# Integer-add weight conversion, a new order of the attention steps, and expert steps inside the last attention units, in a fused attention and two-expert-layer kernel

## The chip, the cores and the metric

The kernel runs on one core of a Trainium2 chip. The metric is the device time of one execution in microseconds (us); the shown time is the median of three runs. One more execution was taken with the hardware profiler, and every duration below comes from it. The engines are PE (matrix multiply; PEld is its weight load), DVE (vector), ACT (scalar, activation), POOL (general purpose) and SP, whose queue starts nearly all DMA transfers.

## The reference

Causal attention with a compressive memory is followed by two feed-forward layers; all three are computed in float32 or better.

```python
B, H, S, D = (4, 8, 576, 64)
scores = scale * np.matmul(q, k.transpose(0, 1, 3, 2))      # causal mask, softmax -> a
local = np.matmul(a, v)
mem_out = einsum(phi(q), M_prev) / (einsum(phi(q), z_prev) + 1e-06)
attn = g * mem_out + (1 - g) * local                        # g = sigmoid(beta) by head
x = attn.transpose(0, 2, 1, 3).reshape(2304, 512)
h = x @ w_in;   x1 = (h * np.cos(h)) @ w_out                # w_in 512 x 2048, w_out 2048 x 512
h = x1 @ w2_in; out = (np.maximum(h, 0.0) ** 2) @ w2_out
```

The four weight matrices are float64. The kernel gets them as pairs of 32-bit words and makes float32 of them itself.

## The kernel before, in words

**Attention** is 16 units (4 batches by 4 pairs of heads). A unit's instructions are written out by hand: `CFG['order']` is a list of tokens such as `S1/2` or `c7/0`. One pass of the loop over u at the end of `attention` (`for u in range(first, end)`) goes through the list, and token T/d issues part T for unit u+d. `_Pinned` keeps each engine's instructions in exactly this order. S are the score matmuls (tile `sps`), R the masked row maxima (tiles `P`, `mx`), E the exponentials, Ns the sums (`sm`), Np the normalisation of P, PT the transposes (`ptps`, `PT`), V and PV the products with the values (`o`), q1 to q6 and qp the memory branch, X the result's way out (`x<-o`, then a store to `xT` in DRAM). In the profile all of these have line L47, that of `_Pinned`, so they are told apart by tile.

**One weight block is converted in each unit**, tokens c1 to c9. `c_load` brings a 128 x 512 block of float64 words (tile `wraw`, two buffers), and `c_steps` has seven operations: absolute value of the high word (ACT), clamp (DVE in attention, POOL later), shift and mask (DVE), sign (DVE, tile `wb`), the exponent (DVE, `wa<-wb`), low word times exponent (DVE, `wa<-wraw,wa`), and the add of the two (POOL, `wa<-wa,wb`). Eight of the 16 blocks are split into a high and a low part that stay on chip, eight are stored to DRAM.

**The expert layers** (`moe`) are 160 steps s, 80 for each layer, one block of up to 512 tokens and 128 hidden columns each. `l1` does 12 matmuls into tile `h`; `g_a` to `g_g` do the activation on ACT and DVE and split it into `gh` and `gl`; `l2`, 12 matmuls, follows two steps later (`SK`). Here no order is pinned: a scheduler sets each engine's order. Between the steps run the conversions of the remaining 48 blocks, one per step for the first layer's last 16 blocks, then blocks of the second layer at `CFG['rate']` = 0.2 per step (these are stored to DRAM, tiles `ws2in` and `ws2out`, and brought back later), and the rest one per step from s = 64 on. The scheduler moves the conversions that have a rate up: 11 of them run in the stretch from 344 to 417 us, through two buffers of `wa` and `wb`. `store` frees a buffer when its transfer has landed.

**The hand-over.** The first expert block's four x parts (`load_x`: `x_load`, then `x_split` with `xh` on ACT, `xl` on DVE) are loaded and split at the end of the pass u = 12. The first `l1` can be issued after `attention` has returned, and the four `h` buffers of `ps_h` lie in space that the attention's pools give back.

Of the kernel before, what the change touches and what calls it, by code (L numbers as in the profile page):

```python
# [32 lines left out]
class _Pinned:  # L33
# [5 lines left out]
    def __getattr__(self, name):  # L39
# [16 lines left out]
CFG = {'order': """  # L56
    R1/1 S0/1 PT1/0 V1/0 Np2/0 PT0/0 c8/-1 R0/1 q5/0 E1/1 q6/0 S2/1 q1/1 PV0/-1 PV3/-1 c2/0 PV2/-1
    E0/1 V0/0 R2/1 PV4/-1 Ns0/1 PV1/-1 PT2/0 S3/1 PT3/0 q2/1 c3/0 V2/0 c4/0 c9/-1 PT4/0 c5/0 qpT/0
    E2/1 R3/1 mem/-1 q3/1 V3/0 Np0/1 Np1/1 V4/0 PT5/0 q4/1 E3/1 c6/0 qpV/0 c7/0 PT6/0 V5/0 X/-1 V6/0
    Ns1/1 S1/2 c1/1 Np3/1  # L60
""",
       'pt': 'AAAAADD',
       'norm': 'PPPA',
       'qpt': 'A',
       'x': 'A',
       'whi': 'A',
       'NA': 4,
       'rate': [0, 0.2, 0.2, 0.2],
       'short': 3,
       'order2': [0, 1, 2, 4, 3],  # L70
       'warm': 8,
       'skew': 2,
       'segs': [[0, 0, 8], [1, 0, 16], [0, 8, 16]],
# [4 lines left out]
def kernel(  # L78
# [62 lines left out]

    def c_steps(raw, clamp=None):
# [4 lines left out]
        af, bf = a.bitcast(F32), b.bitcast(F32)  # L147
# [81 lines left out]

    def attention(ctx):  # L230
        ae = ctx.enter_context(tc.tile_pool(name="ae", bufs=2))
        ac = ctx.enter_context(tc.tile_pool(name="ac", bufs=1))
        a2 = ctx.enter_context(tc.tile_pool(name="a2", bufs=2))
        ps_s = ctx.enter_context(tc.tile_pool(name="ps_s", bufs=2, space=PSUM))
        ps_t = ctx.enter_context(tc.tile_pool(name="ps_t", bufs=2, space=PSUM))
# [394 lines left out]
    def moe(ctx, g_p, g_3):  # L630
        ps_h = ctx.enter_context(tc.tile_pool(name="psh", bufs=4, space=PSUM))
        ps_a = ctx.enter_context(tc.tile_pool(name="psa", bufs=1, space=PSUM))
        hs, rs, kis, gs, acc = {}, {}, {}, {}, {}
        order2 = CFG["order2"]
        segs = [(1, j, a, e) for j, a, e in CFG["segs"]]
        segs += [(1, j, 0, NF) for j in range(2, NB)] + [(2, j, 0, NF) for j in order2]
        steps = [(p, j, f) for p, j, a, e in segs for f in range(a, e)]
        opens = {(p, j, a) for p, j, a, e in segs}
        closes = {(p, j, e - 1) for p, j, a, e in segs}
        xneed, s0 = {}, 0  # L640
        for p, j, a, e in segs:
            if a == 0 and s0:
                for kk in range(KD):
                    xneed.setdefault(max(s0 - 10 + 2 * kk, 0), []).append((p, j, kk))
            s0 += e - a
        part = {}

        def l1(s):
            p, j, f = steps[s]
            n = blocks[j][1]  # L650
            hi, lo = wt[p, "in", f]
            h = ps_h.tile([128, 512], F32, tag="h", name="h")
            for kk in range(KD):
                xh, xl = xt[p, j, kk]
                for x, (lt, rt) in enumerate(((hi, xh), (hi, xl), (lo, xh))):
                    nc.tensor.matmul(  # L656
                        out=h[:, 0:n],
                        lhsT=lt[:, kk * 128:(kk + 1) * 128],
                        rhs=rt[:, 0:n],
                        start=(kk == 0 and x == 0),  # L660
                        stop=(kk == KD - 1 and x == 2),
                    )
            hs[s] = h[:, 0:n]

# [265 lines left out]
```

## Time and profile before

| | |
|---|---|
| runs, us | 1063.88, 1065.28, 1070.35; median 1065.28 |
| profiled execution, us | 1069.46, of which the span is 1067.7 |
| PE busy | 1014.9 us, 95% |
| DVE busy | 700.0 us, 66% |
| ACT busy | 543.6 us, 51% |
| POOL busy | 352.9 us, 33% |
| mean granted PE clock | 0.99 |

The profile's overview cuts the span into 40 slices. PE is at nine tenths or more in nearly all of them, but DVE is at nine tenths in the first fifth of the span, and again from about 600 to 700 us, and PE dips to eight tenths around the hand-over and in the stretch with conversions. So the program has stages with different limits, and each has to be read by itself.

### The profile page before, as it was taken

The numbers are of one execution on the slowest core, as the hardware profiler recorded it, in microseconds if no ns is written. First come the engines' busy times: TensorE is split into PE (matmuls) and PEld (weight loads), VectorE is DVE, ScalarE is ACT, GpSimd is POOL, SyncE is SP. The second block draws the span as 40 slices with busy tenths as digits, with TensorE's granted clock in tenths as the row PEclk, the third lists the DMA queues.
The fourth block names the chain that finished last, engine by engine and source line by source line (L and its number), as shares of the span: only waits on it lengthen the run. The fifth ranks groups of instructions, "written<-read, shape, count | busy, mean of one in ns | idle before, by whom it ended". The sixth has DMA issues, their size and how long they took to land.

```text
span 1067.7 us, 14438 instructions
## 1 busy us (share of the span) xinstructions
PE 1014.9 (95%) x5200; PEld 793.4 (74%) x5200; DVE 700.0 (66%) x1299; ACT 543.6 (51%) x1104; POOL 352.9 (33%) x354
## 2 busy tenths in 40 slices
PE   6999999888999998999999998999999999999998
PEld 4566665566887776888998776777888888888887
DVE  6999998957999888655655899986322422322232
ACT  6888887846655545544565655434222322322222
POOL 5888876658445322000003554663000000000000
PEclk9999999899999999999999999999999999999999
DMA  7555666244222354200203123421100200010010
GB/s 253 154 186 180 193 203 190 81 162 119 89 89 79 119 172 143 71 1 1 80 19 111 59 79 100 136 81 40 59 1 1 70 1 1 10 40 1 1 40 20
DMA packets 53128, 91.65 MB, mean 86 GB/s; under 512 B 7616, under 2 KB 27456, under 8 KB 53056
## 3 DMA queue, kind: packets, MB, share of 16 engines
q1 hardware_dynamic: 52624, 90.23, 26.5%
q8 instruction: 41, 0.67, 0.3%
q10 hardware_dynamic: 432, 0.49, 0.1%
q14 instruction: 31, 0.25, 0.1%
HBM read 71.05 MB, written 19.66 MB: 85 GB/s over the span
## 4 chain that ended last, share of the span: by engine, by line
PE 47%; DVE 32%; issue 6%; DMA 6%; ACT 4%; POOL 4%; SPq 0%; ACTq 0%; POOLq 0%; DVEq 0%
PE a L731 24%; PE h L656 24%; DVE wa L47 4%; DVE P L47 4%; DVE gl L710 3%; DVE wb L157 3%; DVE wa L163 2%; POOL wa L166 2%; DVE wa L153 2%; DMA ws2in<-wa 2%; DVE wa L160 2%; DVE wb L47 1%; DVE gf L677 1%; DVE mn L47 1%; DVE gf L698 1%
## 5 line engine op out<-in xcount | busy, mean ns | idle before, releaser
L656 PE MATMUL h<-xh,winh 128*128 128x512 f32 (+1 forms) x640 | 239.3, 374 | 5.9 <-DVE gf L698 4.3
L656 PE MATMUL h<-xl,winh 128*128 128x512 f32 (+1 forms) x640 | 238.7, 373 | 0.0
L656 PE MATMUL h<-xh,winl 128*128 128x512 f32 (+1 forms) x640 | 238.5, 373 | 0.0
L710 DVE TENSOR_TENSOR gl<-gf,gh 128x512 fp32r<-128x512 f32 (+1 forms) x156 | 114.3, 733 | 126.5 <-ACT gh L703 126.2
L703 ACT ACTIVATE gh<-gf 128x512 fp32r<-128x512 f32 (+1 forms) x160 | 94.0, 587 | 154.1 <-PE a L731 113.4
L656 PEld LDWEIGHTS h<-xh,winh 128*128 128x128 f32 x640 | 120.7, 189 | 30.2 <-DVE gf L698 5.2
L681 DVE TENSOR_TENSOR gf<-gf 128x512 f32<-128x512 f32 (+1 forms) x80 | 60.2, 752 | 120.1 <-ACT gf L673 120.1
L656 PEld LDWEIGHTS h<-xl,winh 128*128 128x128 f32 x640 | 120.8, 189 | 23.0
L656 PEld LDWEIGHTS h<-xh,winl 128*128 128x128 f32 x640 | 120.7, 189 | 22.8
L731 PE MATMUL a<-gl,wouth 128*128 128x512 f32 (+1 forms) x320 | 118.6, 376 | 9.0 <-DVE gl L710 9.0
L731 PE MATMUL a<-gh,woutl 128*128 128x512 f32 (+1 forms) x320 | 117.0, 372 | 0.0
L731 PE MATMUL a<-wouth,gl 128*128 128x512 f32 x288 | 113.6, 394 | 1.2 <-DVE gl L710 1.2
L731 PE MATMUL a<-wouth,gh 128*128 128x512 f32 x288 | 112.8, 393 | 0.6 <-DVE ob L128 0.6
L731 PE MATMUL a<-woutl,gh 128*128 128x512 f32 x288 | 112.7, 391 | 0.0
L673 ACT ACTIVATE gf<-h 128x512 f32<-128x512 f32 (+1 forms) x80 | 44.1, 551 | 118.7 <-PE h L656 118.7
L731 PE MATMUL a<-gh,wouth 128*128 128x512 f32 (+1 forms) x320 | 96.7, 376 | 6.3 <-ACT gh L703 4.9
L166 POOL TENSOR_TENSOR wa<-wa,wb 128x512 f32<-128x512 f32 x48 | 69.1, 1440 | 82.7 <-DVE wa L163 82.7
L691 ACT ACTIVATE gf<-gf 128x512 f32<-128x512 f32 (+1 forms) x80 | 47.0, 587 | 89.2 <-DVE gf L685 89.0
L47 POOL TENSOR_SCALAR P<-P,sm 128x512 f32<-128x512 f32 (+3 forms) x128 | 76.6, 616 | 26.5 <-DVE sm L47 12.1
L698 DVE TENSOR_TENSOR gf<-h,gf 128x512 f32<-128x512 f32 (+1 forms) x80 | 50.7, 634 | 52.4 <-ACT gf L692 52.2
L47 PE MATMUL sps<-qk 64*128 64x384 f32 (+4 forms) x320 | 66.9, 465 | 14.3 <-DVE mx L47 12.0
L731 PEld LDWEIGHTS a<-gl,wouth 128*128 128x128 f32 x320 | 60.6, 189 | 24.0 <-DVE gl L710 13.4
(95 smaller groups left out, 1725.3 us busy)
## 6 DMA issues: line engine op xcount, KB each, us to landing
wraw<-in_moe_w_in_dram SPq DMA_DIRECT2D x32, 512.0 KB, 3.8
wraw<-in_moe_w_out_dram SPq DMA_DIRECT2D x32, 512.0 KB, 3.6
qk<-in_qk_dram SPq DMA_DIRECT2D x15, 640.0 KB, 4.8
qr<-in_qrow_dram SPq DMA_DIRECT2D x16, 320.0 KB, 3.0
vr<-in_vrow_dram SPq DMA_DIRECT2D x16, 320.0 KB, 3.0
xT<-x SPq DMA_DIRECT2D x16, 288.0 KB, 4.5
out_dram<-ob SPq DMA_DIRECT2D x17, 256.0 KB, 2.1
x1T<-ob SPq DMA_DIRECT2D x16, 256.0 KB, 2.5
```

The lines of the kernel that those rows point to most:

```text
L47: made = call(*args, **kwargs)
L153: lambda: dve.tensor_scalar(out=a, in0=a, scalar1=3, scalar2=0x3FFFFFF8, op0=ALU.logical_shift_left, op1=ALU.bitwise_and,),
L157: lambda: dve.scalar_tensor_tensor(out=b, in0=hi, scalar=-0x40000000, in1=a, op0=ALU.bitwise_and, op1=ALU.bitwise_or),
L166: lambda: pool.tensor_tensor(out=af, in0=af, in1=bf, op=ALU.add),
L656: nc.tensor.matmul(out=h[:, 0:n], lhsT=lt[:, kk * 128:(kk + 1) * 128], rhs=rt[:, 0:n], start=(kk == 0 and x == 0), stop=(kk == KD - 1 and ...
L673: nc.scalar.activation(out=rs[s], in_=hs[s], func=AF.Relu)
L681: nc.vector.tensor_tensor(out=rs[s], in0=rs[s], in1=rs[s], op=ALU.mult)
L691: nc.scalar.activation(out=rs[s], in_=rs[s], func=AF.Abs)
L698: nc.vector.tensor_tensor(out=rs[s], in0=hs[s], in1=rs[s], op=ALU.mult)
L703: nc.scalar.activation(out=gh, in_=rs[s], func=AF.Copy)
L710: eng.tensor_tensor(out=gl, in0=rs[s], in1=gs[s].bitcast(F32), op=ALU.subtract)
L731: nc.tensor.matmul(out=o, lhsT=lt, rhs=rt, start=((p, j, f) in opens and x == 0), stop=((p, j, f) in closes and x == 2),)
```

## The change

It has six parts.

1. **Conversion.** The low word is rounded to an integer by ACT (new tile `wc`, scale 2^-29), and DVE adds it to the high part as an integer. The two DVE operations that made the exponent and the product, and POOL's add, are gone. In attention `wc` has two buffers, later one. A unit's block is loaded two units ahead and no longer one.
2. **Order.** The list of tokens is another; `norm` moves the fourth normalisation (Np3) from ACT to POOL.
3. **The x parts** of the first expert block are loaded and split one per pass in the passes u = 8 to 11 (`XL`), each load one pass ahead of its split.
4. **Expert steps 0 to 2** of `l1` are issued inside the last units: step 0 at two S tokens that have no unit left, step 1 in two halves at the next two, step 2 at the head of pass 16.
5. **Rate** 0.4 and no longer 0.2: 18 blocks and no longer 11 are converted in the stretch after the first layer's own conversions, in steps 14 to 28 (16 of them stored), and 13 or 14 and no longer 20 or more are left for the steps from 72 on.
6. **The tile `h`** comes from the attention's pool `ps_s`: one tile of two banks for an even step and the odd one behind it, two tiles in all, where there were four tiles of one bank.

```diff
-    R1/1 S0/1 PT1/0 V1/0 Np2/0 PT0/0 c8/-1 R0/1 q5/0 E1/1 q6/0 S2/1 q1/1 PV0/-1 PV3/-1 c2/0 PV2/-1
+    S0/1 c5/1 R1/1 PT0/0 PT1/0 X/-2 E1/1 q5/0 S2/1 PV0/-1 R0/1 R2/1 V1/0 PV2/-1 PV1/-1 q1/1 V0/0
...
-       'norm': 'PPPA',
+       'norm': 'PPPP',
...
-       'rate': [0, 0.2, 0.2, 0.2],
+       'rate': [0, 0.4, 0.4, 0.4],
...
+        r = (rest or wr).tile([128, DM], I32, tag="wc", name="wc", bufs=2 if rest else 1)
...
-            lambda: dve.tensor_scalar(
-                out=a, in0=b, scalar1=-0x00800000, scalar2=None, op0=ALU.bitwise_and
-            ),
-            lambda: dve.scalar_tensor_tensor(
-                out=af, in0=lo.bitcast(U32), scalar=2.0 ** -52, in1=af, op0=ALU.mult, op1=ALU.mult
-            ),
-            lambda: pool.tensor_tensor(out=af, in0=af, in1=bf, op=ALU.add),
+            lambda: act.activation(out=r, in_=lo.bitcast(U32), func=AF.Copy, scale=2.0 ** -29),
+            lambda: dve.tensor_tensor(out=a, in0=b, in1=r, op=ALU.add),
...
+        if s % 2 == 0 and kks[0] == 0:
+            pair[0] = ps_s.tile([128, 2, 512], F32, tag="s", name="h")
+        h = pair[0][:, s % 2, :]
...
-            conv_load(u + 1)
-            for t, d in steps:
+            if u in (-1, 0):
+                conv_load(u + 1)
+            if 0 <= u - XL < KD:
+                x_split(1, 0, u - XL, xraws.pop())
+            if 0 <= u + 1 - XL < KD:
+                xraws.append(x_load(1, 0, u + 1 - XL))
+            if u == NU:
+                l1(2)
+            for t, d in program:
+                if t[0] == "S" and u + d == NU:
+                    n = len(fill)
+                    fill.append(n)
+                    l1(n // 2, ((0, 1), (2, 3))[n % 2])
...
-            if u == NU - 4:
-                for kk in range(KD):
-                    load_x(1, 0, kk)
...
-            if cur:
+            if cur and s >= early:
                 l1(s)
...
-            for op in ops[0:2]:
+            for op in (ops[0], ops[4], ops[1]) if ops else ():
                 op()
...
-            for op in ops[3:]:
+            for op in (ops[3], ops[5]) if ops else ():
                 op()
```

The order of DVE in one attention unit, before, from the conversion's shift (`wa<-wa`) to the copies of the transposed P (`ISA` rows are the custom operations of the trace):

```order
L47 TENSOR_SCALAR wa<-wa 128x512
L47 SCALAR_TENSOR_TENSOR wb<-wraw,wa 128x512
L47 TENSOR_SCALAR wa<-wb 128x512
L47 ISA Pl_121,mx<-sps,maskl 128x576
L47 ISA mx 128x1
L47 SCALAR_TENSOR_TENSOR qp<-qr,e 128x640
L47 SCALAR_TENSOR_TENSOR wa<-wraw,wa 128x512
L47 COPY PT<-ptps 128x2x128
```

and after:

```order
L47 TENSOR_SCALAR wa<-wa 128x512
L47 SCALAR_TENSOR_TENSOR wb<-wraw,wa 128x512
L47 ISA Pl_121,mx<-sps,maskl 128x576
L47 ISA mx 128x1
L47 SCALAR_TENSOR_TENSOR qp<-qr,e 128x640
L47 ISA wa<-wb,wc 128x1024
L47 COPY PT<-ptps 128x2x128
```

Two operations of the conversion are gone and one, on twice as many elements, stands where the product stood; the operations around them keep their places.

The order of PE around the end of the last attention unit, before (`ptps` are transposes, `o` products of attention, `h` the first expert steps):

```order
L47 MATMUL o<-qpT,mbd_104 128x512
L47 MATMUL o<-qpT,mbd_104 128x64
L47 MATMUL ptps<-ident,P_0_1_114 128x128
L47 MATMUL ptps<-ident,P_1_1_118 128x128
L47 MATMUL ptps<-ident,Pl_122 128x128 x2
L47 MATMUL ptps<-ident,Pl_122 64x128
L656 MATMUL h<-xh_2191,winh_392 128x512
L656 MATMUL h<-xl_2192,winh_392 128x512
L656 MATMUL h<-xh_2191,winl_456 128x512
L656 MATMUL h<-xh_2197,winh_392 128x512
```

and after, with the second half of expert step 1 among them:

```order
L47 MATMUL ptps<-ident,P_0_3_116 128x128
L47 MATMUL ptps<-ident,P_1_3_120 128x128
L47 MATMUL ptps<-ident,Pl_122 128x128 x2
L47 MATMUL h<-xh_1762,winh_669 128x512
L47 MATMUL h<-xl_1763,winh_669 128x512
L47 MATMUL h<-xh_1762,winl_671 128x512
L47 MATMUL h<-xh_1918,winh_669 128x512
L47 MATMUL h<-xl_1919,winh_669 128x512
L47 MATMUL h<-xh_1918,winl_671 128x512
L47 MATMUL o<-qpT,mbd_104 128x512
L47 MATMUL o<-qpT,mbd_104 128x64
L47 MATMUL ptps<-ident,P_0_0_113 128x128
```

Before, the expert's matmuls begin after these transposes; after, steps 0 and 1 are in front of and between them, and step 2 stands before the last unit's products with the values.

The order of ACT in the stretch of conversions, before, with what each instruction waits for (`wa` is the conversion, `ki`, `gf` and `gh` the activation):

```order
L149 ACTIVATE wa<-wraw 128x512 [waits DMAHW6_49,DMAHW5_49,Pool_49]
L692 ACTIVATE gf<-gf,halfpi 128x512 [waits Activation_49]
L671 ACTIVATE ki<-h 128x512 [waits PE_49]
L703 ACTIVATE gh<-gf 128x512 [waits DVE_49]
L691 ACTIVATE gf<-gf 128x512 [waits DVE_49]
L149 ACTIVATE wa<-wraw 128x512 [waits DMAHW7_49,DMAHW0_49,Pool_49]
L692 ACTIVATE gf<-gf,halfpi 128x512 [waits Activation_49]
L671 ACTIVATE ki<-h 128x512 [waits PE_49]
```

and after:

```order
L711 ACTIVATE gh<-gf 128x512 [waits DVE_49,PE_49]
L151 ACTIVATE wa<-wraw 128x512 [waits DMAHW2_49,DMAHW1_49]
L162 ACTIVATE wc<-wraw 128x512 [waits DVE_49]
L679 ACTIVATE ki<-h 128x512 [waits DVE_49]
L711 ACTIVATE gh<-gf 128x512
L151 ACTIVATE wa<-wraw 128x512 [waits DMAHW4_49,DMAHW3_49]
L679 ACTIVATE ki<-h 128x512 [waits PE_49]
L699 ACTIVATE gf<-gf 128x512 [waits DVE_49,Activation_49]
L162 ACTIVATE wc<-wraw 128x512 [waits DVE_49,Activation_49]
```

Before, one conversion stands in five or six instructions of ACT; after, each has two instructions, `wa` and `wc`, two conversions start within eight instructions, and `wc`, of which there is one buffer, waits for DVE.

## Rows read from the trace of the kernel before

**Rows 1.** Busy time by engine in eight stretches; (x) counts instructions.

```profile
core 0: us, PE busy (x) PEld busy (x) DVE busy (x) ACT busy (x) POOL busy (x), PEclk, DMA share, GB/s
75.00:175.00 100.00, 94.21 (x711) 60.72 (x712) 98.39 (x280) 87.00 (x223) 77.53 (x92) 1.00 0.60 190
175.00:200.00 25.00, 20.25 (x120) 12.42 (x119) 21.88 (x51) 17.72 (x46) 16.18 (x18) 0.86 0.51 164
200.00:225.00 25.00, 21.07 (x159) 15.01 (x158) 21.36 (x50) 16.45 (x38) 15.18 (x19) 0.93 0.28 92
225.00:275.00 50.00, 44.07 (x204) 33.59 (x203) 35.31 (x45) 29.77 (x52) 32.07 (x27) 0.97 0.40 119
275.00:325.00 50.00, 50.00 (x218) 40.58 (x217) 47.64 (x66) 29.39 (x50) 27.05 (x22) 1.00 0.31 101
325.00:425.00 100.00, 91.62 (x374) 70.09 (x373) 84.42 (x130) 51.80 (x89) 35.80 (x33) 0.98 0.39 128
600.00:725.00 125.00, 116.88 (x492) 91.12 (x491) 117.95 (x142) 62.06 (x106) 72.16 (x58) 1.00 0.31 97
750.00:850.00 100.00, 100.00 (x435) 81.31 (x434) 30.34 (x44) 27.19 (x45) 0.00 (x0) 1.00 0.09 31
```

**Rows 2.** DVE by shape, 75 to 175 us, eight units: busy us, mean ns, idle before.

```profile
L47 DVE TENSOR_SCALAR wa<-wa 128x512 f32<-128x512 f32 x8 | 11.9, 1483 | 0.0
L47 DVE CUSTOM_DVE_ANT_0 P<-sps,mask 128x512 f32<-128x512 f32 x16 | 10.4, 686 | 0.0
...
L47 DVE TENSOR_SCALAR wa<-wb 128x512 int32<-128x512 int32 x8 | 6.4, 804 | 0.3
...
L47 DVE SCALAR_TENSOR_TENSOR wa<-wraw,wa 128x512 f32<-128x512 uint32 x8 | 5.4, 678 | 0.0
...
L47 DVE CUSTOM_DVE_ANT_0 P<-sps,mask 128x128 f32<-128x128 f32 x16 | 3.9, 280 | 0.0
L47 DVE TENSOR_SCALAR e<-qr 128x640 f32<-128x640 f32 x8 | 3.5, 432 | 0.0
```

**Rows 3.** Timeline of DVE and POOL in one unit: start us, us.

```profile
115.27 1.92 POOL L47 TENSOR_TENSOR e<-qp,zb 128x640 f32<-128x640 f32 x1 [0.76 <-DVE qp L47]
...
116.57 0.64 DVE L47 SCALAR_TENSOR_TENSOR sm<-sm,iom 128x5 f32<-128x5 f32 x1
```

**Rows 4.** ACT by shape, 75 to 175 us.

```profile
L47 ACT ACTIVATE Pl<-Pl,sm 128x576 f32<-128x576 f32 x8 | 6.2, 775 | 6.6 <-DVE sm L47 6.6
...
L47 ACT ACTIVATE wa<-wraw 128x512 f32<-128x512 f32 x8 | 5.4, 674 | 0.0
```

**Rows 5.** POOL by shape, 75 to 175 us.

```profile
L47 POOL TENSOR_SCALAR P<-P,sm 128x512 f32<-128x512 f32 x16 | 14.3, 907 | 9.3 <-PE sps L47 9.3
...
L47 POOL TENSOR_TENSOR wa<-wa,wb 128x512 f32<-128x512 f32 x8 | 10.1, 1269 | 0.0
```

**Rows 6.** Waits, 175 to 225 us: total us, times, longest.

```profile
PE ptps L47 <- ACT PT L47: 6.6, 4, 2.5
...
ACT xh L221 <- DMA xraw<-xT: 4.1, 1, 4.1
```

**Rows 7.** ACT, 340 to 425 us: the weight conversions' first operation.

```profile
L149 ACT ACTIVATE wa<-wraw 128x512 f32<-128x512 f32 x11 | 7.3, 664 | 12.7 <-DMA ws2in<-wa 10.1 <-DMA ws2out<-wa 2.6
```

**Rows 8.** Tile ws2in, 330 to 430 us: a converted block's store to DRAM.

```profile
L187 SPq DMA_DIRECT2D ws2in<-wa x5: 319/326/425, 354.2 to 413.4; - x5
...
DMA to landing us min/median/max: 3.0/4.7/6.0
```

**Rows 9.** DVE, 600 to 725 us: one operation of a conversion.

```profile
L163 DVE SCALAR_TENSOR_TENSOR wa<-wraw,wa 128x512 f32<-128x512 uint32 x19 | 16.6, 875 | 0.4
...
L160 DVE TENSOR_SCALAR wa<-wb 128x512 int32<-128x512 int32 x19 | 12.3, 647 | 0.4
```

**Rows 10.** Timeline of one step of the second expert layer.

```profile
799.77 0.60 ACT L673 ACTIVATE gf<-h 128x512 f32<-128x512 f32 x1 [2.23 <-PE h L656]
...
803.12 0.69 DVE L710 TENSOR_TENSOR gl<-gf,gh 128x512 fp32r<-128x512 f32 x1 [2.03 <-ACT gh L703]
```

More of the change, by code (lines that the diff above doesn't have):

```diff
@@ L71 @@
        'warm': 8,
+       'xl': 8,
        'skew': 2,
@@ L220, in x_split @@
         lo = xs.tile([128, 512], F32R, tag=f"xl{kk}", name=f"xl{kk}")
-        nc.scalar.activation(out=hi[:, 0:n], in_=raw[:, 0:n], func=AF.Copy)
-        nc.vector.tensor_tensor(
+        act.activation(out=hi[:, 0:n], in_=raw[:, 0:n], func=AF.Copy)
+        dve.tensor_tensor(
             out=lo[:, 0:n], in0=raw[:, 0:n], in1=hi[:, 0:n].bitcast(F32), op=ALU.subtract
@@ L225, in x_split, with l1 @@
         xt[phase, j, kk] = (hi, lo)
-    def load_x(phase, j, kk):
-        x_split(phase, j, kk, x_load(phase, j, kk))
+    ps_s = ctx.enter_context(tc.tile_pool(name="ps_s", bufs=2, space=PSUM))
+    hs = {}
+    pair = [None]
+    order2 = CFG["order2"]
+    segs = [(1, j, a, e) for j, a, e in CFG["segs"]]
+    segs += [(1, j, 0, NF) for j in range(2, NB)] + [(2, j, 0, NF) for j in order2]
+    steps = [(p, j, f) for p, j, a, e in segs for f in range(a, e)]
+    opens = {(p, j, a) for p, j, a, e in segs}
+    closes = {(p, j, e - 1) for p, j, a, e in segs}
+    xneed, s0 = {}, 0
+    for p, j, a, e in segs:
+        if a == 0 and s0:
+            for kk in range(KD):
+                xneed.setdefault(max(s0 - 10 + 2 * kk, 0), []).append((p, j, kk))
+        s0 += e - a
+    def l1(s, kks=range(4)):
+        p, j, f = steps[s]
+        n = blocks[j][1]
+        hi, lo = wt[p, "in", f]
+        if s % 2 == 0 and kks[0] == 0:
+            pair[0] = ps_s.tile([128, 2, 512], F32, tag="s", name="h")
+        h = pair[0][:, s % 2, :]
+        for kk in kks:
+            xh, xl = xt[p, j, kk]
+            for x, (lt, rt) in enumerate(((hi, xh), (hi, xl), (lo, xh))):
+                pe.matmul(
+                    out=h[:, 0:n],
+                    lhsT=lt[:, kk * 128:(kk + 1) * 128],
+                    rhs=rt[:, 0:n],
+                    start=(kk == 0 and x == 0),
+                    stop=(kk == KD - 1 and x == 2),
+                )
+        hs[s] = h[:, 0:n]
     def attention(ctx):
@@ L590, in conv_load @@
                 what, kd, f = todo.pop()
-                tiles[n] = [what, kd, f, *c_steps(c_load(wsrc[kd, 1], kd, f), dve)]
+                tiles[n] = [what, kd, f, *c_steps(c_load(wsrc[kd, 1], kd, f), dve, a2)]
         def conv(n, x):
             what, kd, f, wf, ops = tiles[n][:5]
-            if x <= 7:
+            if x <= 6:
                 ops[x - 1]()
-                if x == 7 and what == "spill":
+                if x == 4:
+                    conv_load(n + 2)
+                if x == 6 and what == "spill":
                     store(1, kd, f, wf)
@@ L610, in attention @@
         }
-        steps = [(t.split("/")[0], int(t.split("/")[1])) for t in CFG["order"].split()]
-        first, end = -max(d for _, d in steps), NU - min(d for _, d in steps)
+        program = [(t.split("/")[0], int(t.split("/")[1])) for t in CFG["order"].split()]
+        first, end = -max(d for _, d in program), NU - min(d for _, d in program)
+        XL, xraws, fill = CFG["xl"], [], []
         for u in range(first, end):
@@ L624, in attention, with moe @@
                         emit[t[:-1]](u + d, int(t[-1]))
-            if u == NU - 4:
-                for kk in range(KD):
-                    load_x(1, 0, kk)
         pe, act, dve, pool = nc.tensor, nc.scalar, nc.vector, nc.gpsimd
-    def moe(ctx, g_p, g_3):
-        ps_h = ctx.enter_context(tc.tile_pool(name="psh", bufs=4, space=PSUM))
+    def moe(ctx, g_p, g_3, early):
         ps_a = ctx.enter_context(tc.tile_pool(name="psa", bufs=1, space=PSUM))
[L633 to L663, printed above, removed]
+        rs, kis, gs, acc, part = {}, {}, {}, {}, {}
         def g_a(s):
@@ L876 @@
         wpool[f] = wB
-    moe(ctx, g_p, g_3)
+    moe(ctx, g_p, g_3, len(hs))
 _INS = ['M_prev', 'z_prev', 'beta', 'moe_w_in', 'moe_w_out', 'moe2_w_in', 'moe2_w_out']
```

11 lines of the change are left out of this document (5 added, 6 removed).

## Prediction

> **What bounds the kernel now.** I read the busy time by engine and stretch first, since one share over the whole span hides the stages. From 75 to 175 us, in steady attention, DVE is busy 98.39 of 100 us, PE 94.21, ACT 87.00, POOL 77.53 [rows 1]: DVE is the bound, and PE stands 4 us behind it. Those 100 us hold eight units (eight clamps, rows 2), so 12.5 us each, of which DVE works 98.39/8 = 12.3 and PE 94.21/8 = 11.8. From 275 to 325 and from 750 to 850 us PE is busy all the time, with 218 and 435 matmuls; 435 in 100 us, so 0.23 us each and 24 x 0.23 = 5.5 us for a full expert step, is PE's own pace, which nothing in this change alters.
>
> So the question is where PE falls short of that pace. Rows 1 show five places: attention itself; 175 to 200 us, with PE busy 20.25 of 25 and a granted clock of 0.86; the hand-over from 200 to 275 us, idle for 3.93 + 5.93 = 9.9 us; 325 to 425 us, where 374 matmuls ran and not 435, so 61 x 0.23 = 14.0 us are lost; and 600 to 725 us, 492 and not 544, 12.0 us. From 750 us on there is nothing to gain.
>
> **The change part by part.** The sum is made against the profiled execution, 1069.5 us (its span is 1067.7). That is 4.2 us above the median shown, 1065.3, and I take the same difference off the median.
>
> *Conversion in attention.* Per unit DVE loses two operations, 0.804 + 0.678 = 1.48 us [rows 2]. It gains an integer add that the trace does not show. The order lists it as a custom operation on 1024 elements, two 16-bit halves of each word. The nearest rows are the custom maxima, 0.686 us for 512 elements and 0.280 for 128 [rows 2]: 0.406/384 = 1.06 ns per element, so 0.686 + 512 x 0.00106 = 1.23 us for 1024. If both halves of a word go at once it is that of 512, 0.69. I take 1.23, as the order counts elements; DVE then saves 0.25 us per unit, or 0.79 with the lower price. ACT gains the low-word copy, 0.674 like its neighbour on the same tile, and loses Np3, 0.775 [rows 4]: nothing. POOL loses 1.269 and gains Np3, somewhat above the 0.907 of its 512-wide normalisation [rows 5], about 1.03: POOL falls by 0.24.
>
> There is a second effect. Some DVE operations take far longer than their size: the clamp 1.483 us on 512 elements beside 0.432 for a similar operation on 640 [rows 2], and a product on five elements 0.64, which ends at 117.21, just as POOL's product of 1.92 us, begun at 115.27, ends at 117.19 [rows 3]. POOL is busy 78% [rows 1]. The Trainium skill ("SBUF — State Buffer", "Who interferes with whom") says that GpSimd and a DVE operation in a two-port mode, or with two SBUF inputs, shut each other out for a whole instruction; rows 3 agree with it, 0.64 us for five elements. By that rule the new add, with two inputs, waits as the product did, and POOL's two-input add, now gone, no longer blocks anyone. I count, from the rows alone, a quarter of the clamp's excess of 1.05 us as gained, 0.26, because POOL's work falls little. Together 0.5 us per unit. Bounds: a loss of 0.8 if the add waits 1.05 us each time as the clamp does (1.48 - 1.23 - 1.05), and a gain of 12.5 - 11.8 = 0.7, where PE becomes the bound. Over 14 of the 16 units, the first and the last being mostly filling and draining: **7 us**, from -11 to +10. The new order as such I cost at nothing beyond this: it moves the same parts within a unit that is bound by busy time, not by waits; if it opens waits between engines, the slack that covers them is DVE's 1.6% of idle time, 0.2 us in a unit.
>
> *x parts.* Near 186 us ACT waits 4.1 us for the x transfer, and PE then waits 6.6 us in four pieces for the transposed copies behind it [rows 6]. PE's deficit from 175 to 200 us is 4.75 us idle, less the 1.45 that attention always has, and 0.14 x 25 = 3.5 for the clock of 0.86 that follows the idling: 6.8 us. With each load a pass ahead of its split this wait goes. What is late next is DVE: four splits of about 0.69 (a 512-wide operation, rows 2), 2.8 us, stay in units bound by DVE, as they were. ACT's copies of 0.67 fit in its 13% of idle time. SP's queue carries the same four loads, only earlier. I take **3 us**; bounds 0 and 6.8.
>
> *Hand-over.* Three first-layer steps are 36 x 0.23 = 8.3 us of PE work. They move from behind attention into its last units, where PE idles 3.93 us from 200 to 225 and 5.93 us to 275 [rows 1]. Their covers are the waits for the softmax of the last units; if these are shorter than the matmuls, the last units are delayed instead and nothing is won. With x ready early, the chain from x to the first activation starts earlier too. I take half of the idle 9.9, **5 us**; bounds 0 and 9.
>
> *The packed conversions.* In steps 14 to 28 now run 18 conversions, not 11, in 14.5 steps: 80 us, 4.4 us each. Before, five stores of one tensor began between 354.2 and 413.4 us [rows 8], with four of the other among them: 59.2/8 = 7.4 us per conversion. With two buffers a buffer's round is thus 14.8 us, of which the store takes 4.7 [rows 8] and ACT's first operation 0.66 [rows 7]; ACT waited 12.7 us for stores [rows 7]. The new chain lacks POOL's 1.27 and 0.25 of DVE: 13.3 us, a pace of 6.6. But the old round also held waiting for a turn, since only 12.7 of the 59 us were waits for a store. I take the middle between 6.6 and the order's own 4.4, so 5.5: 18 x 5.5 = 99, less 80, is 19 lost where 14 were lost before: **-5 us**; bounds +14 (at 4.4) and -39 (at 7.4). ACT's queue is what a late store holds up: behind the conversion stand `ki` and `gh`, for which DVE and PE wait.
>
> *The later conversions.* Here DVE is busy 117.95 of 125 us [rows 1]. Some 20 conversions become 14: 12.0 x 14/20 leaves 8.4, so 3.6 won; and DVE's price falls from 0.647 + 0.875 [rows 9] to 1.23, 0.29 for 14, 4.1 us, of which I count two thirds. **6 us**; bounds 2 and 12.
>
> *The paired tile.* An odd step's matmuls now wait until the even step's `h` has been read, and an even step's last read waits for the odd step's matmuls. PE does two l2 blocks, 5.5 us, between; in the second layer the chain from 799.77 to the end of `gl` at 803.81 is 4.0 us [rows 10], and 6 us of other matmuls lie before the step that needs it. **0**; bounds 0 and -8.
>
> Sum: 7 + 3 + 5 - 5 + 6 = 16; 1069.5 - 16 = 1053.5, as a median 1049.
>
> **The rivals.** *Slower: the stores set the pace.* If two buffers still turn over one conversion in 7.4 us, 18 take 133 us, 53 over their steps, 39 more than before; against 21 from the other parts that is 18 lost, a median of 1083. It decides from (14 + 21 + 80)/18 = 6.4 us per conversion. For it: ACT's 12.7 us of waits for stores [rows 7], and a `wc` of one buffer. Against: the chain is shorter.
>
> *No change: the packed stretch eats what the others give.* At 6.2 us, near the scaled pace, 18 x 6.2 - 80 = 32 are lost, 18 more than before; 3 are left: 1062.
>
> *Much faster: the collisions go.* If the add takes 0.69 and the clamp's excess shrinks, attention runs at PE's pace, 10 us; the packed stretch loses no more than before, the later one nothing (12), x 6, hand-over 7: 35, a median of 1030. For it: 1.05 us of excess in one operation per unit. Against: POOL is nearly as busy as before. The Trainium skill ("VectorE: DVE Perf Modes", what auto-detection actually checks) lets a two-source operation on 16-bit data do two elements per cycle. That would be this rival's add; no run shows it yet.
>
> **How the numbers follow.** The forecast, 1049 with its own range of 1040 to 1058, has a chance of 0.43; the slower rival 0.14; no change 0.21; much faster 0.22. About 1% is what a measurement of this kernel can tell from no change: below 1054.6 and above 1076. Three quarters of the forecast's chance, 0.32, and the fast rival's 0.22 make 0.54 faster; slower is 0.14; the rest, 0.32, is the same. The range takes in most of the fast case and stops short of the slow one's middle: 1030 to 1072.
>
> **What would show it.** Right: the add near 1.2 us; a unit near 12.0 us; no wait for x near 186 us; PE idle under 5 us from the last unit to the third step; about 350 matmuls per 100 us in steps 14 to 28, with ACT waiting for stores; DVE below PE after 650 us. Wrong: an add of 0.7, conversions at 4.4 or at 7 us each, or PE waiting for a reader of `h` in the second layer.

## The result, and the profile after

The changed kernel took 1054.97 us (median of four runs), the kernel before 1064.71. One of the four, the profiled one, was disturbed, with a mean granted clock of 0.84 and 1121.97 us, and is left out of the ratio: 0.9889, 95% interval 0.9842 to 0.9936, so 1.1% or 12 us faster. The forecast was 1049 and a gain of 16. The profile after is that of the same kernel run again (the first experiment below), 1054 us with a mean clock of 0.98.

The busy time by stretch, as in [rows 1]:

```profile
core 0: us, PE busy (x) PEld busy (x) DVE busy (x) ACT busy (x) POOL busy (x), PEclk, DMA share, GB/s
75.00:175.00 100.00, 97.05 (x749) 66.11 (x748) 91.33 (x283) 95.29 (x245) 87.82 (x97) 1.00 0.64 210
175.00:200.00 25.00, 23.24 (x182) 15.54 (x179) 21.05 (x68) 21.19 (x56) 21.05 (x24) 1.00 0.42 147
200.00:225.00 25.00, 23.08 (x148) 16.07 (x148) 10.60 (x23) 10.83 (x21) 4.94 (x8) 0.93 0.34 108
225.00:275.00 50.00, 37.18 (x128) 27.84 (x129) 36.44 (x43) 33.63 (x59) 31.25 (x25) 0.83 0.40 121
275.00:325.00 50.00, 48.64 (x210) 38.76 (x208) 43.47 (x65) 36.13 (x64) 21.01 (x19) 1.00 0.35 113
325.00:425.00 100.00, 97.42 (x419) 77.91 (x418) 79.36 (x133) 66.55 (x117) 11.72 (x16) 1.00 0.54 173
600.00:725.00 125.00, 122.55 (x529) 98.85 (x529) 80.05 (x110) 64.37 (x113) 36.42 (x33) 1.00 0.23 72
750.00:850.00 100.00, 100.00 (x433) 81.14 (x433) 29.13 (x43) 25.85 (x43) 0.00 (x0) 1.00 0.05 19
```

Attention is now bound by PE, with 97.05 of 100 us, and ACT, 95.29; DVE has fallen from 98.39 to 91.33. From 175 to 200 us PE ran 182 matmuls and not 120, and the clock stays at 1.00. From 325 to 425 us there are 419 matmuls for 374, from 600 to 725 us 529 for 492, where DVE is down from 117.95 to 80.05. But from 225 to 275 us PE is busy only 37.18 us, where it was 44.07, and its granted clock is 0.83 for 0.97.

The same by stages. Each row is a time read off the trace: the last X copy (`x<-o`), and the end of the matmul that is the 12(s+1)th of l2's line (all of step s done; the last row is the last matmul). In brackets is the length of the stage.

| end of | before, us | after, us | change of the stage |
|---|---|---|---|
| attention (last X starts) | 232.66 | 224.16 | -8.5 |
| step 3 | 269.62 (36.96) | 267.24 (43.08) | +6.1 |
| step 15 | 331.98 (62.36) | 337.15 (69.91) | +7.6 |
| step 31 | 433.53 (101.55) | 428.69 (91.54) | -10.0 |
| step 63 | 568.58 (135.05) | 564.18 (135.49) | +0.4 |
| step 91 | 735.84 (167.26) | 721.57 (157.39) | -9.9 |
| step 159 | 1063.64 (327.80) | 1048.69 (327.12) | -0.7 |

These are single profiled executions, so their sum, -15, is not the measured -12 to the microsecond. It shows where the time went: three stages gain 28 us and the hand-over, from the end of attention to step 15, gives 14 back. The first X copy starts 7 us later after the change (46.67 us and not 39.62), so attention's 8.5 us are won against that.

The operations of a conversion in attention, DVE by shape from 75 to 175 us, answering to [rows 2]:

```profile
L47 DVE CUSTOM_DVE_ANT_0 wa<-wb,wc 128x1024 uint16<-128x1024 uint16 x9 | 6.1, 680 | 0.0
...
L47 DVE TENSOR_SCALAR e<-qr 128x640 f32<-128x640 f32 x8 | 3.9, 488 | 0.0
L47 DVE SCALAR_TENSOR_TENSOR sm<-sm,iom 128x5 f32<-128x5 f32 x8 | 3.4, 421 | 0.0
L47 DVE TENSOR_SCALAR wa<-wa 128x512 f32<-128x512 f32 x8 | 3.4, 420 | 0.0
```

The integer add takes 0.680 us on its 1024 halves, the price of a custom operation on 512 elements. So two halves go at once. The Trainium skill's rule ("VectorE: DVE Perf Modes", "What auto-detection actually checks") that a two-source operation on 16-bit data reaches two elements per cycle agrees with this number. And the clamp takes 0.420 us where it took 1.483.

The store of a packed block, and ACT's waits for it, answering to [rows 8] and [rows 7]:

```profile
L184 SPq DMA_DIRECT2D ws2in<-wa x8: 319/326/455, 324.6 to 389.9; - x8
...
DMA to landing us min/median/max: 3.2/3.5/6.8
```

```profile
L151 ACT ACTIVATE wa<-wraw 128x512 f32<-128x512 f32 x13 | 8.7, 670 | 9.6 <-DMA ws2in<-wa 6.3 <-DMA ws2out<-wa 3.2
```

Eight stores of one tensor begin between 324.6 and 389.9 us. With seven of the other between them, 14 intervals in 65.3 us are 4.7 us each, where it was 7.4. ACT still waits for stores, 9.6 us, but PE loses 100 - 97.42 = 2.6 us in its stretch and not 8.4.

### The profile page after: what moved, and what is told of

Its sections match the earlier page's. It is cut to its first block, busy times and chain, and to the rows that moved or that the text cites. A ratio compares the mean times of both kernels' runs of the same rounds, so it can differ in the third digit from the quotient of the medians.

```text
span 1120.2 us, 14448 instructions
## 1 busy us (share of the span) xinstructions
PE 1088.2 (97%) x5200; PEld 820.3 (73%) x5200; DVE 602.0 (54%) x1235; ACT 567.2 (51%) x1152; POOL 281.0 (25%) x306
## 4 chain that ended last, share of the span: by engine, by line
PE 92%; DVE 3%; DMA 2%; ACT 2%; POOL 0%; issue 0%; SPq 0%; DVEq 0%; ACTq 0%; POOLq 0%
PE a L739 38%; PE h L250 37%; PE o L47 6%; PE sps L47 4%; PE ptps L47 4%; DMA wraw<-in_moe_w_in_dram 1%; PE qps L47 1%; PE h L47 1%; DVE P L47 1%; DVE xl L219 1%; ACT P L47 0%; DMA qk<-in_qk_dram 0%; DVE wb L159 0%; DMA xraw<-xT 0%; POOL P L47 0%
## 5 line engine op out<-in xcount | busy, mean ns | idle before, releaser
L250 PE MATMUL h<-xh,winh 128*128 128x512 f32 (+1 forms) x628 | 246.7, 393 | 4.3 <-DVE gf L706 2.3
L250 PE MATMUL h<-xl,winh 128*128 128x512 f32 (+1 forms) x628 | 246.6, 393 | 0.0
L250 PE MATMUL h<-xh,winl 128*128 128x512 f32 (+1 forms) x628 | 246.2, 392 | 0.0
L718 DVE TENSOR_TENSOR gl<-gf,gh 128x512 fp32r<-128x512 f32 (+1 forms) x156 | 103.7, 665 | 144.0 <-ACT gh L711 143.6
L689 DVE TENSOR_TENSOR gf<-gf 128x512 f32<-128x512 f32 (+1 forms) x80 | 51.9, 653 | 152.8 <-ACT gf L681 152.6
L739 PE MATMUL a<-gh,woutl 128*128 128x512 f32 (+1 forms) x320 | 124.2, 394 | 0.0
L739 PE MATMUL a<-woutl,gh 128*128 128x512 f32 x288 | 120.0, 417 | 0.0
L739 PE MATMUL a<-wouth,gh 128*128 128x512 f32 x288 | 105.8, 417 | 0.0
L679 ACT ACTIVATE ki<-h 128x512 int32<-128x512 f32 (+1 forms) x80 | 44.1, 552 | 87.5 <-DVE gf L706 65.4
L739 PEld LDWEIGHTS a<-gh,wouth 128*128 128x128 f32 x320 | 58.6, 195 | 25.2 <-ACT gh L711 10.9
```

Source lines behind the costliest of these rows:

```text
L250: pe.matmul(out=h[:, 0:n], lhsT=lt[:, kk * 128:(kk + 1) * 128], rhs=rt[:, 0:n], start=(kk == 0 and x == 0), stop=(kk == KD - 1 and x == 2),)
L679: nc.scalar.activation(out=kis[s], in_=hs[s], func=AF.Copy, scale=1.0 / TWO_PI)
L689: nc.vector.tensor_tensor(out=rs[s], in0=rs[s], in1=rs[s], op=ALU.mult)
L718: eng.tensor_tensor(out=gl, in0=rs[s], in1=gs[s].bitcast(F32), op=ALU.subtract)
L739: nc.tensor.matmul(out=o, lhsT=lt, rhs=rt, start=((p, j, f) in opens and x == 0), stop=((p, j, f) in closes and x == 2),)
```

## The experiments

All ratios are to the kernel before, on the same chip. The first four runs below, the next four and the last three were made on three chips, so between these groups the ratios are compared too: a difference of 2 or 3 us in the times is not clear of the noise there.

**The changed kernel again** (no edit).

> The changed kernel again, for a profile at full clock. Theory (the prediction's sum): 1055 us; in attention a unit takes about 12.0 us; the stretch of 18 packed conversions loses about 19 us against PE's pace (4.35 matmuls per us), the later conversions about 6. Rival 1 (collisions of DVE and POOL gone): a unit of 11.8 us or less with DVE idle over 5%, so attention alone gives 10 us or more, and something else gives 5 or more of it back. Rival 2 (stores set the pace): the packed stretch loses 30 us or more.

1054.15 us, ratio 0.9891 [0.9872, 0.9909]. A unit takes 11.56 us (the X copies of five units follow each other at that distance) and not 12.67, up to where the x parts are split; those four units take 13.03, 12.13, 12.13 and 11.80. That is rival 1, with DVE idle 8.7%, but for its size: attention ends 8.5 us earlier, not 10 or more. The unit is shorter than the theory's 12.0, and something gives part of the gain back.

**The rate at 0.2.**

```diff
-       'rate': [0, 0.4, 0.4, 0.4],
+       'rate': [0, 0.2, 0.2, 0.2],
```

> The changed kernel with the rate back at 0.2 (fewer conversions early, more after step 64). Theory: the packed stretch gets 5 us shorter, the later one 4 us longer: within 3 us of the changed kernel. Rival 1 (stores set the pace): 10 us or more faster. Rival 2 (the later conversions are what the rate was for): 8 us or more slower.

1056.69 us, ratio 0.9915 [0.9895, 0.9936]: 2.5 us slower, hardly beyond the spread. That is the theory's total, and neither rival. Its parts are smaller: with the rate at 0.2 steps 16 to 31 take 1.2 us less (90.4 for 91.5), not 5, and steps 64 to 91 1.6 more (158.9 for 157.4), not 4. The packed conversions cost nothing on balance.

**No early expert steps.**

```diff
-            if u == NU:
-                l1(2)
...
-                if t[0] == "S" and u + d == NU:
-                    n = len(fill)
-                    fill.append(n)
-                    l1(n // 2, ((0, 1), (2, 3))[n % 2])
```

> The changed kernel without expert steps 0 to 2 in the last units (issued after attention, as before; the early x parts stay). Theory: 5 us slower, the price that the prediction gave them. Rival (they only delay the last units): within 2 us.

1053.07 us, ratio 0.9885 [0.9865, 0.9906]: 1 us faster than with them, within the spread. The rival holds: beside the pair the early steps are worth nothing.

**No early steps and no pair.**

```diff
-            pair[0] = ps_s.tile([128, 2, 512], F32, tag="s", name="h")
-        h = pair[0][:, s % 2, :]
+        h = ps_h[0].tile([128, 512], F32, tag="h", name="h")
...
+        ps_h.append(ctx.enter_context(tc.tile_pool(name="psh", bufs=4, space=PSUM)))
```

> As the run without the early expert steps, and with h in four tiles of one bank again in place of two of two banks. Theory: the pairing costs nothing, so within 2 us of that run. Rival (PE waits for readers of the pair): 5 us or more faster than that run, and waits of PE for DVE readers of h gone from the profile.

1038.6 us, ratio 0.9748 [0.9732, 0.9764]: 14.5 us faster than with the pair, and the fastest version but one. The rival holds in time. Of the profile it expected too much: PE's waits for DVE readers of `h` are not gone. The waits of PE from 215 to 265 us, first of the changed kernel, then of this run:

```profile
PE a L739 <- ACT gh L711: 8.6, 2, 8.0
PE h L250 <- DVE gf L706: 2.4, 1, 2.4
PE h L250 <- DVE gf L685: 2.3, 1, 2.3
```

```profile
PE h L248 <- DVE gf L700: 5.2, 3, 2.1
```

What is gone is a wait of 8.0 us of l2 for `gh` (5.6 us in two pieces, the longer 4.7, in the run with the pair and without the early steps, which differs in the pair alone). Is `gh` earlier, then? PE and ACT in the run with the pair and without the early steps, from the timeline (`h` is l1, `a` l2; `ki` is the first read of a step's `h`):

```profile
220.47 0.60 ACT L673 ACTIVATE ki<-h 128x512 int32<-128x512 f32 x1 [2.80 <-PE o L47]
...
221.84 0.50 PE L250 MATMUL h<-xh,winh 128*128 128x512 f32 x1 [0.24 <-DVE gf L679]
...
228.41 0.58 ACT L673 ACTIVATE ki<-h 128x512 int32<-128x512 f32 x1
228.89 0.63 ACT L705 ACTIVATE gh<-gf 128x512 fp32r<-128x512 f32 x1
...
229.57 1.94 PE L733 MATMUL a<-gh,wouth 128*128 128x512 f32 x4 [4.71 <-ACT gh L705]
...
229.93 0.59 ACT L673 ACTIVATE ki<-h 128x512 int32<-128x512 f32 x1
...
237.13 0.79 PE L250 MATMUL h<-xh,winh 128*128 128x512 f32 x1 [2.57 <-DVE gf L679]
...
237.71 0.63 ACT L705 ACTIVATE gh<-gf 128x512 fp32r<-128x512 f32 x1 [1.65 <-DVE gf L700]
```

and in the run with neither:

```profile
218.67 0.60 ACT L673 ACTIVATE ki<-h 128x512 int32<-128x512 f32 x1 [3.41 <-PE o L47]
...
222.47 0.58 ACT L673 ACTIVATE ki<-h 128x512 int32<-128x512 f32 x1
...
223.98 0.59 ACT L673 ACTIVATE ki<-h 128x512 int32<-128x512 f32 x1
...
227.83 0.47 PE L248 MATMUL h<-xh,winh 128*128 128x512 f32 x1 [1.59 <-issue]
...
229.16 0.58 ACT L673 ACTIVATE ki<-h 128x512 int32<-128x512 f32 x1
...
229.63 0.62 ACT L705 ACTIVATE gh<-gf 128x512 fp32r<-128x512 f32 x1
...
230.70 1.10 PE L733 MATMUL a<-gh,wouth 128*128 128x512 f32 x4
...
233.40 0.50 PE L248 MATMUL h<-xh,winh 128*128 128x512 f32 x1 [1.60 <-DVE gf L700]
233.47 0.61 ACT L705 ACTIVATE gh<-gf 128x512 fp32r<-128x512 f32 x1
...
238.16 1.10 PE L733 MATMUL a<-gh,wouth 128*128 128x512 f32 x4
```

The first `gh` comes at 228.89 and at 229.63 us, no earlier without the pair. But until the first l2 PE has run 36 matmuls of l1 with the pair, three steps, and then stands, 4.71 us before that l2 and 2.57 before the odd step 3, which waits for DVE's read of step 2. Without the pair it has run 60, five steps, and waits a little for a free buffer. ACT's order differs too: step 1's first read comes 7.9 us after step 0's with the pair, 3.8 without. PE in the same stretch, first with the pair, then without:

```profile
218.00:240.00 22.00, 14.13 (x62) 9.46 (x61) 14.72 (x15) 15.15 (x26) 14.62 (x12) 0.84 0.52 158
```

```profile
218.00:240.00 22.00, 18.81 (x88) 14.49 (x85) 17.16 (x15) 16.08 (x28) 17.47 (x13) 1.00 0.47 136
```

62 matmuls for 88, and a granted clock of 0.84 on the mean for 1.00: 26 x 0.23 = 6 us less of PE's work done.

By stages, the pair costs 7.6 us from the end of attention to step 3 (42.7 against 35.1), 4.1 to step 15, 2.2 to step 31 and 1.5 after. Another 1.8 lie before the end of attention; these two profiled executions are 17.3 us apart, the medians 14.5.

**Early steps 0 and 1 in one pair, single banks from step 2 on.**

```diff
+        if ps_h:
+            h = ps_h[0].tile([128, 512], F32, tag="h", name="h")
+        else:
+            if s % 2 == 0 and kks[0] == 0:
+                pair[0] = ps_s.tile([128, 2, 512], F32, tag="s", name="h")
+            h = pair[0][:, s % 2, :]
...
```

> The changed kernel with h in single banks from step 2 on, and only steps 0 and 1 early, in one pair. Theory (the pairing is the cost, the early steps are worth what the prediction gave them): 1034 us, 4 to 5 below the run with neither. Rival (ACT's and DVE's work sets when the first l2 can start, so the early steps are worth nothing): within 2 us of 1038.6.

1039.29 us, ratio 0.9724 [0.9692, 0.9756]. By the time the rival holds again; the ratio, 0.0024 below that of the run with neither, would also allow the theory's 4 us. The traces decide it: from the first X copy to the end of step 15 this run takes 276.7 us, and the run with neither 276.1. So the early steps are worth nothing with single banks behind them either.

**The kernel before with the new conversion alone.**

```diff
-            lambda: dve.tensor_scalar(
-                out=a, in0=b, scalar1=-0x00800000, scalar2=None, op0=ALU.bitwise_and
-            ),
-            lambda: dve.scalar_tensor_tensor(
-                out=af, in0=lo.bitcast(U32), scalar=2.0 ** -52, in1=af, op0=ALU.mult, op1=ALU.mult
-            ),
-            lambda: pool.tensor_tensor(out=af, in0=af, in1=bf, op=ALU.add),
+            lambda: act.activation(out=r, in_=lo.bitcast(U32), func=AF.Copy, scale=2.0 ** -29),
+            lambda: dve.tensor_tensor(out=a, in0=b, in1=r, op=ALU.add),
...
```

> The kernel before with the new conversion alone (old order, old x parts, rate 0.2, no early steps, single banks). Theory (the conversion gives most of the attention's gain and of the later conversions'): a unit of 11.9 us or less and 15 us or more below the kernel before, so 1050 or less. Rival (the new order gives it): a unit above 12.3 us, 1056 or more.

1046.64 us, ratio 0.9798 [0.9773, 0.9823]: 20 us faster than the kernel before, and more than 7 faster than the whole change. So the theory's total holds, but not its unit: that takes 12.43 us, no better than the rival's. By stages 10.3 us are won up to the end of attention, 10.4 between steps 15 and 31 and 4.9 between 63 and 91; some 3 are lost between the end of attention and step 15. Of the 10.3, 0.24 in each of eleven steady units make 2.7. The largest piece, 4.6, is the distance of two X copies near the end, 8.1 us for 12.7: there PE waits 2.5 and 1.4 us for ACT's and DVE's copies of the transposed P before, and 0.8 us in all in this run.

**The old list of tokens, without early steps and pair.**

```diff
-    S0/1 c5/1 R1/1 PT0/0 PT1/0 X/-2 E1/1 q5/0 S2/1 PV0/-1 R0/1 R2/1 V1/0 PV2/-1 PV1/-1 q1/1 V0/0
...
+    R1/1 S0/1 PT1/0 V1/0 Np2/0 PT0/0 c8/-1 R0/1 q5/0 E1/1 q6/0 S2/1 q1/1 PV0/-1 PV3/-1 c2/0 PV2/-1
...
```

> The changed kernel without early steps and without the pair, with the old list of tokens (the conversion's add on POOL left out of it). Theory: the order as such is worth little, within 4 us of 1038.6. Rival: 8 us or more slower, with attention units longer by 0.5 us.

1040.83 us, ratio 0.9749 [0.9726, 0.9772]: 2.2 us slower than with the new list by the times, on another chip, and the same by the ratios (0.9748). That is the theory's number. But its units are longer by 0.5 to 0.9 us (12.06 to 12.43 and not 11.56), as the rival said. Both are true because the new list also makes the pipeline longer: its first X copy starts at 45.94 us and not at 40.52, its last at 219.83 and not 222.29. The fifteen units between them take 7.9 us less with the new list, and 5.4 of it are paid back by the later start. (Two more runs with the new list and without the pair, at other rates, start at 47.5 and 47.6 us and end attention at 221.4 and 221.7, so even the 2.5 us that remain here are not sure.) DVE by shape from 75 to 175 us with the old list:

```profile
L47 DVE TENSOR_SCALAR wa<-wa 128x512 f32<-128x512 f32 x8 | 11.9, 1483 | 0.0
...
L47 DVE SCALAR_TENSOR_TENSOR sm<-sm,iom 128x5 f32<-128x5 f32 x8 | 9.6, 1202 | 0.0
...
L47 DVE CUSTOM_DVE_ANT_0 wa<-wb,wc 128x1024 uint16<-128x1024 uint16 x8 | 7.9, 985 | 0.0
```

The same operations take 1.483, 1.202 and 0.985 us here, and 0.420, 0.424 and 0.679 in the run with neither, with nothing changed but the order. That is 2.15 us per unit of waiting inside operations (3.67 less 1.52); the unit gains less, since PE and ACT are the bound next. What POOL does beside the clamp, with the old list:

```profile
106.80 1.32 POOL L47 TENSOR_TENSOR qp<-qp,mn 128x640 f32<-128x640 f32 x1 [0.92 <-DVE mn L47]
106.91 1.48 DVE L47 TENSOR_SCALAR wa<-wa 128x512 f32<-128x512 f32 x1
```

and with the new one:

```profile
107.91 0.88 POOL L47 TENSOR_SCALAR P<-P,sm 128x128 f32<-128x128 f32 x1
108.22 0.42 DVE L47 TENSOR_SCALAR wa<-wa 128x512 f32<-128x512 f32 x1
```

With the old list the clamp starts 0.11 us after POOL's product and ends 0.27 us after it. With the new one it stands beside a short normalisation and takes 0.42 us, and it is POOL that is longer: the 128x128 normalisations take 0.623 us on the mean and not 0.376. So a part of the waiting has moved to POOL, where it is cheaper.

**Rate 0.2, without early steps and pair.** On top of those edits:

```diff
-       'rate': [0, 0.4, 0.4, 0.4],
+       'rate': [0, 0.2, 0.2, 0.2],
```

> The changed kernel without early steps and without the pair, rate 0.2. Theory: the packed conversions cost nothing, the later ones cost some, as in the run with the pair: 2 to 3 us slower than 1038.6. Rival: packed conversions cost once PE isn't held by the pair: 4 us or more faster.

1041.08 us, ratio 0.9747 [0.9723, 0.9772]: 2.5 us slower by the times, which is the theory, and the same by the ratios, so the total is not clear of the noise; the rival, 4 us faster, is not seen. In the traces steps 18 to 31 take 78.5 us for 80.7, steps 64 to 91 160.1 for 156.5: seven more conversions early cost 2.2 us and save 3.6.

**The kernel before with the pair alone.**

```diff
-        ps_h = ctx.enter_context(tc.tile_pool(name="psh", bufs=4, space=PSUM))
+        ps_h = ctx.enter_context(tc.tile_pool(name="psh", bufs=2, space=PSUM))
+        pair = [None]
...
-            h = ps_h.tile([128, 512], F32, tag="h", name="h")
+            if s % 2 == 0:
+                pair[0] = ps_h.tile([128, 2, 512], F32, tag="h", name="h")
+            h = pair[0][:, s % 2, :]
```

> The kernel before with the pair of banks for h alone (two tiles of two banks). Theory (the pair costs by itself, most of it at the hand-over and up to step 15, where DVE and ACT are late): 10 us or more slower than the kernel before, 1076 or more. Rival (it costs only beside the new conversions, which crowd ACT): within 4 us of the kernel before.

1082.25 us, ratio 1.0138 [1.0114, 1.0161]: 15 us slower than the kernel before. The pair costs by itself, in both kernels about the same. Where in the kernel before it costs them is not shown: no reading of this run's trace is given.

**The pair, with l1 of both steps issued together.**

```diff
-            if cur and s >= early:
-                l1(s)
+            if cur and s % 2 == 0:
+                l1(s)
+                l1(s + 1)
...
```

> The changed kernel without early steps, with the pair, but l1 of the even and of the odd step issued together, so that no odd l1 waits for a reader of the even step's h; the even step's readers wait for both. Theory (PE stands in its queue behind an odd l1 that waits for DVE): most of the 14.5 us comes back, 1045 or less. Rival (the late reads of the even step are the cost): 1050 or more.

1054.33 us, ratio 0.9879 [0.9861, 0.9897]: in total nothing comes back, so the theory that most of the loss is PE standing behind an odd l1 falls. PE's waits over the whole span:

```profile
PE h L250 <- DVE gf L700: 13.9, 9, 2.8
...
PE a L733 <- ACT gh L705: 6.1, 3, 4.2
```

Now `h` waits 13.9 us, in nine pieces, for `gf` (L700), the last reader of a pair; without the pair that wait is 6.1 us in four. A buffer is free only when both of its steps have been read for the last time, so the loss has in part changed its place. PE's waits in l1 and l2 (`h` and `a`) for DVE's `gf` and ACT's `gh` sum to 20.0 us here, 18.3 with the pair and each l1 by itself, and 8.7 without the pair.

By stages there is more to see. The runs of the changed kernel with the new list differ in how many matmuls of l1 PE has done when the first l2 starts:

| run | l1 matmuls before the first l2 | first X copy to end of step 15, us |
|---|---|---|
| the changed kernel, and with the rate at 0.2 | 36 | 290.5, 288.5 |
| pair, no early steps | 36 | 289.8 |
| pair, l1 issued together | 48 | 284.6 |
| neither, at three rates | 60 | 276.1 to 276.2 |
| steps 0 and 1 early in a pair, single banks behind | 72 | 276.7 |

With l1 issued together 5.2 us do come back up to step 15, and 3.7 are lost again behind it (steps 64 to 91 take 162.0 us for 158.3). In the last row step 1's first read comes 8.0 us after step 0's, as late as in the runs with the pair, and nothing is lost. So it is not this late read that costs the time at the start; in these runs the loss goes with how far PE can run ahead.

**Rate 0.6, without early steps and pair.**

```diff
-       'rate': [0, 0.4, 0.4, 0.4],
+       'rate': [0, 0.6, 0.6, 0.6],
```

> The changed kernel without early steps and without the pair, rate 0.6. Theory (each conversion moved ahead of step 64 saves there more than it costs early, 2.5 us for the step from 0.2 to 0.4): 1 to 2 us below 1038.6. Rival (the early stretch is full at 0.4): 2 us or more above it.

1038.11 us, ratio 0.9728 [0.9713, 0.9743]: 0.5 us below the run at 0.4 by the times, 2 by the ratios, within the spread. The rival is not seen and the theory's 1 to 2 us cannot be told from nothing: what is saved late (steps 64 to 91 take 154.5 us) is paid early (82.2 from 18 to 31). It has the shortest time, 2.7% below the kernel before, where the change as made gives 1.1%; the other versions of the changed kernel without the pair lie within 3 us of it.

## Why the prediction was right or wrong

The time was near and the side right, but by terms that do not hold one by one: errors of both signs cancelled, and the nearness was luck. Two of the prediction's own signs of being wrong came: an add of 0.7 us, and conversions near 4.4 us each.

*Conversion in attention, 7 us, and x parts, 3.* Together 10 were forecast; attention ends 8.5 us earlier. The sum is near, but the conversion's prices are not. The add was sized at 1.23 us and takes 0.680, the other bound. With the old order that alone would have given 1.48 - 0.69 = 0.79 per unit; it gave 12.67 - 12.43 = 0.24, because the waits moved into the operations that stayed. In the run with the new conversion alone the add takes 0.985 us, the five-element `sm` 1.201 (0.648 before), and `qp` 0.814 (1.085 before): 1.48 - 0.985 - 0.55 + 0.27 = 0.22. Even so this run ends attention 10.3 us earlier, more than the whole change does, since most of the gain is not in the equal units that the sum counted but in the last ones.

*The order, nothing.* For the unit the step "the new order as such I cost at nothing" fails: the list is what takes the clamp from 1.483 to 0.420 and the unit from 12.43 to 11.56. For the time it was nearly right, 2.2 us or less, because the later start is paid once. "POOL is nearly as busy as before" was weighed against the collisions' going. POOL is busier, 87.82 of 100, and DVE's collisions are gone or shorter all the same, so it is not how much POOL works but beside what. The rule of the Trainium skill on the ports that DVE and GpSimd share ("SBUF — State Buffer", "Who interferes with whom": the operation that starts second waits for the whole of the first) fits the clamp that ends just after POOL's product; the two runs that differ in nothing but the list are its test here. Beside a normalisation that had started first, though, it was not the clamp that took longer.

*The x parts* came near their price: the two long units of 17.96 and 13.58 us between X copies, 6.2 above the 12.67 of the others, have become four that are above 11.56 by 1.5, 0.6, 0.6 and 0.2, 2.9 in all; 3.3 won for the 3. No run varies them alone. Their reasoning has one reading wrong: of the 6.6 us in [rows 6], 4.0 in three pieces lie near 186 us, and the piece of 2.5 is the one in the last units that the new conversion removes.

*Hand-over, +5, and the paired tile, 0.* These were wrong by 19: the stage from attention to step 15 is 13.7 us longer. The pair makes 11.7 of it (7.6 and 4.1), and the run with the new conversion alone, without the pair, is 2.9 longer there too. The step "the paired tile: 0; bounds 0 and -8" failed. It looked at the steady steps, where there is room (the stages from step 31 to 63 and behind 91 show +0.4 and -0.7), and not at the start, where ACT, DVE and POOL are all late and PE lives on the steps of l1 that it can run ahead: five with four single buffers, three with the pair. The price is 14.5 us by the pair of runs, and 15 in the kernel before. "I take half of the idle 9.9" failed too: the early steps move PE's work, and the first l2 waits for ACT's chain behind it whatever PE did before. With the pair they lose 1 us, and without it they win nothing up to step 15.

*The packed conversions, -5.* They gained: the stage is 10.0 us shorter. The pace was taken as 5.5, between 4.4 and 6.6, and is 4.7, near the order's own. The failing step is to scale the old round of 14.8 us by the durations that went. In the run with the new conversion alone, with the same rate and the same nine stores as before, the stores follow each other at 4.6 us and no longer 7.4, and the stretch is 10.4 us shorter; so it was the old conversion's operations more than the stores that set the old pace. The slower rival, with the stores as the bound, falls with that; ACT still waits 9.6 us for stores, while PE loses 2.6 us in the stretch.

*The later conversions, 6.* 9.9; 4.9 of them come with the conversion alone, and 1.6 with the rate. Mis-sized with the add.

*The rivals.* The much faster one named the right mechanism, collisions gone and an add of 0.69, and its 1030 is near what the kernel reaches without the pair, 1038. The pair was bounded at 8 and never made a rival, which it should have been.

Open: why the scheduler puts step 1's first read later with the pair, and why issuing l1 together loses in steps 64 to 91 what it wins at the start. Both are seen in the traces, neither was varied alone.

## What to carry to other kernels

A buffer made of two halves is waited for and freed as a whole: ask not only whether the steady state has room, but how many steps ahead the fill-up at the start of a stage ran on single ones. Work moved earlier on one engine gained nothing here, where another engine's chain starts the next stage. Before pricing an instruction taken off a bound engine, see how much of its neighbours' time is waiting for another engine, since that wait may simply move to the next operation; then the order decides what the shorter count is worth. And look at the first and the last units of a pipeline by themselves: here they held more of the gain than the steady ones.

## What was not expected of the hardware

A DVE operation on 128 x 512 float words takes 0.420 or 1.483 us, and one on five elements 0.424 or 1.202, in programs that differ in the order of their instructions alone. A custom add on 1024 halves of words costs what a custom operation on 512 words costs, 0.680 us beside 0.686. And the granted clock, a mean of 0.83 from 225 to 275 us in the changed kernel, where PE waits 8.0 us, is 1.00 in that stretch in the run with neither early steps nor pair, where that wait is missing. The mean is a mix of two levels, 1.00 (2.4 GHz) and 0.50 (1.2 GHz). Three stretches of the changed kernel:

```profile
225.00:230.00 5.00, 0.00 (x0) 0.00 (x0) 1.76 (x3) 4.97 (x9) 4.59 (x4) 0.93 0.59 169
230.00:235.00 5.00, 2.72 (x6) 1.72 (x7) 4.10 (x5) 5.00 (x10) 5.00 (x5) 0.50 0.48 154
255.00:260.00 5.00, 5.00 (x13) 3.93 (x12) 4.79 (x8) 1.82 (x4) 1.93 (x2) 0.50 0.35 101
```

PE ran nothing from 225 to 230 us, and in the next 5 us the clock was 0.50. From 255 to 260 us PE is busy all the time at 0.50, and does 13 matmuls; in the next 5 us, at 1.00, it does 23. The run with neither:

```profile
225.00:275.00 50.00, 42.27 (x178) 32.54 (x177) 45.13 (x52) 36.17 (x64) 31.81 (x26) 1.00 0.40 119
```
